# A windowed-attention and FFN kernel: one list scheduler from slot 28 on, with POOL in its model, and the softmax division moved behind the values

## The chip, the cores and the metric

One core of a Trainium2 chip runs the whole program. The metric is the device time of one execution in microseconds; three runs of the kernel before give 895.34 us as median.

The engines are named as the profile names them: PE multiplies matrices and PEld loads its weights, DVE is the vector engine, ACT the scalar (activation) engine, POOL the GpSimd engine, and SP only issues DMAs. Each engine works through its own instruction list strictly in order; an instruction that waits holds up everything behind it on its engine.

## What is computed

```python
# q, k, v: 8 batches x 8 heads x 576 positions x 64
scores = q @ k.T / 8
# heads 0-3 see the last 32 positions, heads 4-7 every 4th of the last 128
scores = where(mask, scores, -1e9)
attn = exp(scores - max); attn = attn / (sum(attn) + 1e-9)
x = (attn @ v) laid out as 4608 tokens x 512
h = x @ w_in                          # 512 x 2048
g = max(h, 0) + log1p(exp(-abs(h)))   # softplus
out = g @ w_out                       # 2048 x 512
```

Everything is float32 to the outside. PE multiplies in a reduced form, so that every operand is split into a high part (a cast, on ACT) and a low part (a subtraction, on DVE) and each product is three matmuls: high x high, low x high, high x low.

## The kernel before

**Tokens and stages.** The 4608 tokens are 9 chunks of 512. Chunks 0 to 2 go through a plain FFN in 48 *slots*: a slot is one 128-wide slice of the 2048 (`ff`) for one chunk, 12 matmuls of w_in (tile `h_ps`), the softplus on ACT and DVE (`e`, then the high part `gh` and the low part `gl`), and, two slots later, 12 matmuls of w_out (tile `o_ps`). `RUNS` sets the order: slots 26 to 31 end chunk 1, slots 32 to 47 are chunk 2. Chunks 3 to 8 go in three *supers* of two chunks each, with Strassen's scheme in the form with seven products: a super is an H half (28 *units* for w_in) and an O half (28 units for w_out), and a unit is 12 matmuls of 128x128x512. The seven products are listed in `PRODUCTS`, named by their left operand: a11, a12 and a22 are blocks of x (or of g in the O half), s1 to s4 are sums of blocks that POOL makes. In an H half the seven products follow one another within each of four column blocks `jj`; in an O half each product runs over the four `jj` before the next begins. Their results go to three pairs of PSUM banks x, y and z, from which ACT and DVE take them (`temp`, `g_of`).

**What an O half costs beside its matmuls.** Each of its 28 units needs its operand split: a cast on ACT (L1100) and a 128x1024 subtraction on DVE (L1181, tile `g`) into one of three pairs of buffers `moving`. For s2, s3 and s4 POOL adds or subtracts a 128x1024 block (L1108), four for each, and four times already in the H half. The weights of a unit come by DMA into a ring of five buffers (`load_unit`).

**Attention.** Two head pairs (a *group* each) make a *couple*; chunk c has the groups 4c to 4c+3, so two couples a chunk, named by the number of their first group. For each group from chunk 2 on: PE makes the scores (`s_ps`), DVE scales, masks and takes the maximum (L380, L385), POOL subtracts the maximum (`shifted`, L388), ACT takes one exponential over 128x512 (L395), DVE sums (L413) and inverts, POOL multiplies by the inverse (`divide`, L421), DVE turns 32x32 squares (L443, `sq`), and SP sends them to DRAM in four DMAs (`turned`) and fetches them back (`pt`). Then PE makes the values (`a_ps`), DVE turns them (L537), and SP sends and fetches x the same way (`rows`, `x_full`). Scores and values share one pair of PSUM banks, and PE takes either as a *visit* of 128 small matmuls.

**Weight jobs.** The sums of weight blocks for the supers are made on the chip: 16 `weight_job`s, each six POOL operations (L818, L834), two casts, two DVE subtractions (L842) and four DMAs (`w_t`).

**What sets the order.** Slots 0 to 9 are written out by hand (`OPENING`). Slots 10 to 47 have a queue of events with due times written by hand (`at`, `attend`, `weight_job`). The supers are ordered by a list scheduler: every piece of work is a `Task` with an engine, a cost and the keys it reads and writes; at each step the engine that can start first runs its most urgent task, by the latest start that its followers allow. POOL is there one more engine; that a POOL operation and a DVE operation can hold each other up is not in the model.

```python
1249            task("DVE", 1.05, gr.divisor, reads=s, writes=[("ri", e)])
1250            task("POOL", 1.05, gr.divide, reads=[("ri", e)], writes=s)
1251            task("DVE", 0.65, turn, n + e, reads=s, writes=[f"q{e}"])
1252            task("SP", 0.4, send, n + e, reads=[f"q{e}"], writes=[("sent", e)], size=QK // 2)
...
1285        done.latest = 5.5 + u * UNIT
```

## Time and profile before

| what | value |
|---|---|
| median of 3 runs | 895.34 us (895.1 to 898.06) |
| the profiled execution, its own time | 893.6 us |
| its span, first to last instruction | 891.8 us |
| PE busy | 829.2 us (93%) |
| DVE busy | 684.6 us (77%) |
| ACT busy | 494.1 us (55%) |
| POOL busy | 344.7 us (39%) |
| mean granted clock of PE | 0.978 |

The last is the share of full speed that the chip granted PE, averaged over the span; where it is 0.50 in a stretch, matmuls run at half their pace. A PE that is drawn as busy need not be at full pace, since the ends of matmuls are modelled. What tells is how long a stage takes for the matmuls in it. The stages, from the span's start: slot 28's first matmul is at 210.2 us, the three H halves begin at 365.2, 548.0 and 728.4, the three O halves at 450.2, 633.7 and 804.5, and the last matmul ends near 887.4.

### The profile page before, as it was taken

To read this page: it belongs to the slowest core of one execution; us is meant where nothing else is said; L and a number is where in the kernel's file an instruction comes from. 1 tells how busy PE (TensorE), PEld (TensorE's weight loads), DVE (VectorE), ACT (ScalarE), POOL (GpSimd) and SP (SyncE) were. 2 spreads that over 40 slices of the span, in tenths; PEclk is the share of its full clock that TensorE was granted. 3 is DMA by queue.
4 is the path that set the end of the run, shared out by engine and by line. 5 is a ranking of instruction groups with operands and counts; after the bars stand their busy time and mean duration, and the time that the engine had idled before them with its cause. 6 is when DMAs were issued, how large, how long until landed. Compare 5 with 4: busy or idle time off the path is not lost.

```text
span 891.8 us, 19364 instructions
## 1 busy us (share of the span) xinstructions
PE 829.2 (93%) x7834; PEld 660.5 (74%) x7835; DVE 684.6 (77%) x872; ACT 494.1 (55%) x767; POOL 344.7 (39%) x218
## 2 busy tenths in 40 slices
PE   6799999899789888999999898899998799999998
PEld 4578888787567776778877676788876588887876
DVE  5798998897586777678799787687896846778663
ACT  5687666555454455467763342586743517775341
POOL 0000101047687879224366342243483502225700
PEclk9899999999899998999999999999999999999999
DMA  9499277989878743897887885969878656664573
GB/s 335 161 354 384 69 212 260 326 252 324 261 245 278 260 152 135 278 343 251 297 286 241 277 295 151 348 215 344 275 255 259 227 199 199 195 190 162 168 239 115
DMA packets 118473, 218.93 MB, mean 245 GB/s; under 512 B 11504, under 2 KB 53616, under 8 KB 118384
## 3 DMA queue, kind: packets, MB, share of 16 engines
q1 hardware_dynamic: 117952, 216.97, 73.1%
q8 instruction: 62, 1.02, 0.5%
q10 hardware_dynamic: 432, 0.72, 0.2%
q14 instruction: 27, 0.22, 0.1%
HBM read 162.07 MB, written 55.57 MB: 244 GB/s over the span
## 4 chain that ended last, share of the span: by engine, by line
PE 62%; DVE 15%; POOL 8%; issue 5%; ACT 5%; DMA 3%; SPq 1%; DVEq 0%; POOLq 0%; ACTq 0%
PE y L208 15%; PE z L208 13%; PE h_ps L208 10%; PE o_ps L208 10%; PE x L208 7%; DVE g L1181 6%; PE s_ps L208 3%; PE a_ps L208 3%; DMA pt<-turned 2%; POOL x_full L878 1%; ACT e L1111 1%; POOL b L818 1%; DVE a_l L890 1%; SPq L143 1%; ACT g L1100 1%
## 5 line engine op out<-in xcount | busy, mean ns | idle before, releaser
L1108 POOL TENSOR_TENSOR g_of<-g_of 128x1024 f32<-128x1024 f32 x36 | 96.5, 2683 | 201.3 <-DVE g_of L1114 179.2
L1181 DVE TENSOR_TENSOR g<-g_of,g 128x1024 fp32r<-128x1024 f32 x72 | 118.2, 1649 | 36.4 <-ACT g L1100 36.4
L208 PE MATMUL h_ps<-xh,parts 128*128 128x512 f32 x384 | 133.2, 404 | 5.6 <-DVE e L655 5.6
L208 PE MATMUL o_ps<-gh,parts 128*128 128x512 f32 x384 | 133.2, 404 | 4.5 <-DVE ob L726 4.2
L1100 ACT CAST g<-g_of 128x1024 fp32r<-128x1024 f32 x72 | 75.4, 1047 | 111.1 <-PE y L208 48.7
L208 PE MATMUL y<-g,ring 128*128 128x512 f32 x432 | 108.9, 406 | 14.5 <-DVE g L1181 14.5
L388 POOL TENSOR_TENSOR s<-s,nm 128x512 f32<-128x512 f32 x28 | 34.9, 1252 | 208.2 <-DVE nm L385 177.1
L208 PEld LDWEIGHTS y<-g,ring 128*128 128x128 f32 x432 | 82.1, 193 | 38.5 <-DVE g L1181 19.7
L1111 ACT ACTIVATE e<-e 128x1024 f32<-128x1024 f32 x96 | 102.0, 1062 | 2.7
L208 PEld LDWEIGHTS h_ps<-xh,parts 128*128 128x128 f32 x384 | 74.3, 193 | 24.1 <-DVE e L655 6.9
L208 PEld LDWEIGHTS o_ps<-gh,parts 128*128 128x128 f32 x384 | 73.5, 191 | 23.3 <-ACT e L649 4.6
L208 PE MATMUL o_ps<-gl,parts 128*128 128x512 f32 x192 | 77.3, 403 | 3.2 <-DVE gl L670 3.2
L208 PE MATMUL h_ps<-xl,parts 128*128 128x512 f32 x192 | 76.8, 400 | 0.0
L208 PE MATMUL z<-g,ring 128*128 128x512 f32 x288 | 70.5, 402 | 5.0 <-DVE g L1181 5.0
L1105 DVE TENSOR_TENSOR temp<-y,temp 128x512 f32<-128x512 f32 x60 | 40.4, 686 | 38.9 <-PE y L208 35.6
L208 PE MATMUL x<-g,ring 128*128 128x512 f32 x288 | 68.4, 395 | 1.0 <-DVE g L1181 1.0
L208 PEld LDWEIGHTS z<-g,ring 128*128 128x128 f32 x288 | 54.6, 191 | 19.6 <-DVE g L1181 6.9
L1114 DVE SCALAR_TENSOR_TENSOR g_of<-g_of,e 128x1024 f32<-128x1024 f32 x36 | 60.8, 1694 | 9.7 <-ACT e L1111 9.5
L208 PEld LDWEIGHTS x<-g,ring 128*128 128x128 f32 x288 | 53.8, 188 | 14.0 <-DVE g L1181 1.4
L208 PE MATMUL x<-a_h,ring 128*128 128x512 f32 x192 | 63.4, 391 | 0.0
L208 PE MATMUL y<-s_h,ring 128*128 128x512 f32 x192 | 63.3, 391 | 0.0
L208 PE MATMUL z<-s_h,ring 128*128 128x512 f32 x192 | 63.2, 390 | 0.0
(94 smaller groups left out, 1634.5 us busy)
## 6 DMA issues: line engine op xcount, KB each, us to landing
ring<-w_t SPq DMA_DIRECT2D x96, 512.0 KB, 4.9
ring<-w_b SPq DMA_DIRECT2D x72, 512.0 KB, 4.3
raw<-w SPq DMA_DIRECT2D x64, 256.0 KB, 5.4
w_t<-cast SPq DMA_DIRECT2D x64, 256.0 KB, 3.4
v<-vp SPq DMA_DIRECT2D x28, 512.0 KB, 5.1
w_b<-parts SPq DMA_DIRECT2D x48, 256.0 KB, 4.6
q<-qp SPq DMA_DIRECT2D x36, 256.0 KB, 5.6
turned<-sq SPq DMA_DIRECT2D x112, 64.0 KB, 2.0
```

What stands on the lines that cost most here:

```text
L143: ins = tc.keep_in_program_order((engine or nc.sync).dma_start(**kw))
L208: tc.keep_in_program_order(nc.tensor.matmul(**kw))
L388: pin(nc.gpsimd.tensor_tensor(out=self.blocks, in0=self.blocks, in1=self.nm.unsqueeze(2).to_broadcast([P, NB, WKEYS]), op=ALU.add))
L818: pin(nc.gpsimd.tensor_tensor(out=sums[j].rearrange("p k n -> p (k n)"), in0=parts[:, 0], in1=parts[:, 1], op=ALU.add))
L878: pin(nc.gpsimd.tensor_tensor(out=dst, in0=a, in1=b, op=op))
L890: pin(nc.vector.tensor_tensor(out=low, in0=x_of(first, name), in1=high.bitcast(F32), op=ALU.subtract))
L1100: pin(nc.scalar.copy(out=dst, in_=src))
L1105: pin(nc.vector.tensor_tensor(out=dst, in0=a, in1=b, op=ALU.add))
L1108: pin(nc.gpsimd.tensor_tensor(out=dst, in0=a, in1=b, op=op))
L1111: pin(nc.scalar.activation(out=dst, in_=src, func=func, **kw))
L1114: pin(nc.vector.scalar_tensor_tensor(out=dst, in0=src, scalar=0.0, in1=e, op0=ALU.max, op1=ALU.add))
L1181: lambda: pin(nc.vector.tensor_tensor(out=low, in0=src, in1=high.bitcast(F32), op=ALU.subtract)),
```

## The change

1. From slot 28 on (`PLANNED`) everything is one list of tasks: the last 20 slots, ten of the weight jobs, the couples and the supers. The due times by hand for that stretch are gone. Two weight jobs stay by hand, and the last four (`LATE_JOBS`) move into the first super. The weight blocks of w_out that are stored unchanged (24 DMAs) move from hand-set times in slots 14 to 28 into the list.
2. The model's costs are new, and a DVE task marked `port` that starts while POOL works is charged up to twice its cost.
3. For all unmasked groups (chunk 2 on) `shifted` and the sum on DVE go; instead ACT takes eight exponentials of 128x64 with the maximum as bias and the sum as accumulated output, as it did for chunks 0 and 1.
4. For couples from 14 on, `divide` on POOL goes; `normalized` multiplies the values by the inverse on DVE, reading PSUM, between the values and their turning.
5. Couples overlap: the scores of a couple are asked for ahead of the values of the one before. From couple 16 on the queries and every second `v` lie in the half of x that the couple will fill, and the fetched squares lie where q lay.
6. The seven products are reordered, s1 second, and the banks with them; in the O half s3 is made in place.

```diff
     PRODUCTS = (
-        ("a11", "b11"), ("s2", "t2"), ("a12", "b21"), ("s3", "t3"), ("s1", "t1"), ("a22", "t4"), ("s4", "b22"),
+        ("a11", "b11"), ("s1", "t1"), ("s2", "t2"), ("a12", "b21"), ("s3", "t3"), ("s4", "b22"), ("a22", "t4"),
     )
...
-        def shifted(self):
-            pin(nc.gpsimd.tensor_tensor(
-                out=self.blocks, in0=self.blocks, in1=self.nm.unsqueeze(2).to_broadcast([P, NB, WKEYS]), op=ALU.add
-            ))
-
-        def exponentials(self):
-            self.sm = wk.tile([P, NB], F32, name="sm")
-            if not self.masked:
-                pin(nc.scalar.activation(out=self.s, in_=self.s, func=AF.Exp))
-                return
-            for t in range(NB):
+        def exponentials(self, some=range(NB)):
+            if 0 in some:
+                self.sm = wk.tile([P, NB], F32, name="sm")
+            for t in some:
...
+        def normalized(self):
...
+            pin(nc.vector.tensor_tensor(
+                out=rows.rearrange("p (h m d) -> p h m d", h=2, d=D),
+                in0=self.rows.rearrange("p h t (r d) -> p h (t r) d", d=D),
+                in1=self.ri.rearrange("p (h m) -> p h m", h=2).unsqueeze(3).to_broadcast([P, 2, 4, D]),
+                op=ALU.mult,
+            ))
...
+    for i in range(OPENED + 1, PLANNED):
...
+    COST = {
+        "PE": 0.2275, "ACT": (0.24, 0.00079), "DVE": (0.16, 0.00104), "POOL": (0.12, 0.00245),
+    }
...
+    @sooner
+    def weights(n, begun=False):
+        x = x_of_couple(n)
+        queries = ["q0", "q1"] if begun else [x]
...
+        Task("PE", 1.4, lambda: scores(n), [*queries, "k0", "k1"], ["att"], visit=True)
+        for e in range(2):
+            gr, s = groups[n + e], both("s") if e == 0 else [("s", 1)]
+            task("DVE", (512, 512), gr.maximum, reads=["att"], writes=s)
+            s = [("s", e)]
+            for t in range(0, NB, 2):
+                Task("ACT", 1.07, lambda gr=gr, t=t: gr.exponentials(range(t, t + 2)), (), s)
...
+    def couples(first, last):
+        for n in range(first, last, 2):
+            weights(n)
+            if n > first:
+                attended(n - 2)
+            turned(n)
+        attended(last - 2)
...
+    for i in range(PLANNED, LAST + 1):
+        if slots[i] == (2, 0):
+            for n in range(BY_HAND, 2 * NPAIR - LATE_JOBS):
+                sooner(job, JOBS_SOONER)(n // NPAIR, n % NPAIR, False)
+        early_slot(i)
+        if slots[i] == (2, LAG):
+            couples(2 * NPAIR, 2 * NPAIR + 4)
...
+            cost = t.cost
+            if t.port and t.engine == "DVE":
+                cost += min(cost, max(0.0, free["POOL"] - start))
```

How the instructions stand, at three places.

POOL, from the last weight job into the halves of the first super; `b` and `d` are a weight job's, `x_full<-x_full` the sums for x of a super, `s<-s,nm` is `shifted`, `s<-s,ri` is `divide`, `g_of<-g_of` the sums of g blocks. Before:

```order
L834 TENSOR_TENSOR b<-b,d 128x256
L834 TENSOR_TENSOR b<-b 128x256
L388 TENSOR_TENSOR s<-s,nm 128x512 x2
L421 TENSOR_TENSOR s<-s,ri 128x512 x2
L1108 TENSOR_TENSOR g_of<-g_of 128x1024 x2
L388 TENSOR_TENSOR s<-s,nm 128x512 x2
L421 TENSOR_TENSOR s<-s,ri 128x512 x2
L1108 TENSOR_TENSOR g_of<-g_of 128x1024 x4
```

After:

```order
L1076 TENSOR_TENSOR b<-parts 128x512 x2
L1076 TENSOR_TENSOR d<-b 128x256 x2
L1076 TENSOR_TENSOR b<-b,d 128x256
L1076 TENSOR_TENSOR b<-b 128x256
L1076 TENSOR_TENSOR b<-parts 128x512 x2
L1076 TENSOR_TENSOR g_of<-g_of 128x1024
L1076 TENSOR_TENSOR d<-b 128x256 x2
L1076 TENSOR_TENSOR b<-b,d 128x256
L1076 TENSOR_TENSOR b<-b 128x256
L1076 TENSOR_TENSOR g_of<-g_of 128x1024 x15
L897 TENSOR_TENSOR x_full<-x_full 128x1024 x4
L1076 TENSOR_TENSOR g_of<-g_of 128x1024 x16
```

The attention's work is gone from POOL, and the last of the jobs (the end of four of them is seen here) lie around the first sum of the first super's H half.

DVE, the last slots before the first unit; `e<-h_ps,e` is the end of a slot's softplus and `gl` its low part, `cast` belongs to weight jobs, `s_l` to the x of the first super. Before:

```order
L655 SCALAR_TENSOR_TENSOR e<-h_ps,e 128x512
L890 TENSOR_TENSOR a_l<-x_full,a_h 128x1024
L842 TENSOR_TENSOR cast<-d,cast 128x2x256
L670 TENSOR_TENSOR gl<-e,gh 128x512
L890 TENSOR_TENSOR s_l<-x_full,s_h 128x1024
L842 TENSOR_TENSOR cast<-b,cast 128x2x256
L890 TENSOR_TENSOR s_l<-x_full,s_h 128x1024
L655 SCALAR_TENSOR_TENSOR e<-h_ps,e 128x512
```

After:

```order
L679 SCALAR_TENSOR_TENSOR e<-h_ps,e 128x512
L694 TENSOR_TENSOR gl<-e,gh 128x512
L1229 TENSOR_TENSOR cast<-b,cast 128x2x256
L679 SCALAR_TENSOR_TENSOR e<-h_ps,e 128x512
L1229 TENSOR_TENSOR cast<-b,cast 128x2x256
L694 TENSOR_TENSOR gl<-e,gh 128x512
L909 TENSOR_TENSOR a_l<-x_full,a_h 128x1024
L679 SCALAR_TENSOR_TENSOR e<-h_ps,e 128x512
L909 TENSOR_TENSOR s_l<-x_full,s_h 128x1024
L694 TENSOR_TENSOR gl<-e,gh 128x512
```

Between `e` and the next `gl` there stood two other subtractions, and now at most one; between two slots' `e`, `gl` apart, there stood five, and now at most two.

DVE, the first super's O half, where the splits `g` of its units alternate with attention. Before:

```order
L1181 TENSOR_TENSOR g<-g_of,g 128x1024
L413 TENSOR_REDUCE sm<-s 128x8
L415 TENSOR_SCALAR sm<-sm 128x8
L418 RECIPROCAL ri<-sm 128x8
L1181 TENSOR_TENSOR g<-e,g 128x1024
L413 TENSOR_REDUCE sm<-s 128x8
L415 TENSOR_SCALAR sm<-sm 128x8
L418 RECIPROCAL ri<-sm 128x8
L443 STREAM_TRANSPOSE sq<-s 128x512
L1181 TENSOR_TENSOR g<-e,g 128x1024
```

After:

```order
L1076 TENSOR_TENSOR g<-g_of,g 128x1024
L536 TENSOR_TENSOR normal<-a_ps,ri 128x512 x2
L449 STREAM_TRANSPOSE sq<-s 128x512 x2
L419 TENSOR_SCALAR sm<-sm 128x8
L424 RECIPROCAL ri<-sm 128x8
L419 TENSOR_SCALAR sm<-sm 128x8
L424 RECIPROCAL ri<-sm 128x8
L1076 TENSOR_TENSOR g<-g_of,g 128x1024
L393 SCALAR_TENSOR_TENSOR s<-s_ps,mask 128x512
L398 TENSOR_REDUCE nm<-s 128x8
```

The sum is gone, the inverse stands behind the turning of the squares instead of ahead of it, and the multiplication `normal` has come in.

## Rows read from the trace of the kernel before

**Rows 1.** E, then H, O alternating: length; busy PE, PEld, DVE, ACT, POOL; clock.
```profile
210.20:365.20 155.00, 136.03 (x1274) 107.39 (x1272) 111.97 (x128) 76.98 (x126) 117.16 (x99) 0.93 0.72 234
365.20:450.20 85.00, 83.29 (x850) 68.30 (x849) 67.66 (x99) 56.91 (x66) 29.61 (x18) 1.00 0.86 286
450.20:548.00 97.80, 88.43 (x849) 68.37 (x849) 87.56 (x73) 41.06 (x44) 51.83 (x22) 0.98 0.75 252
548.00:633.70 85.70, 83.34 (x850) 68.02 (x850) 63.81 (x91) 55.23 (x63) 26.23 (x14) 1.00 0.85 287
633.70:728.40 94.70, 86.24 (x722) 67.94 (x721) 74.06 (x61) 40.37 (x43) 45.91 (x18) 0.98 0.73 246
728.40:804.50 76.10, 76.10 (x337) 63.02 (x336) 50.87 (x61) 52.52 (x59) 14.44 (x6) 1.00 0.63 200
804.50:887.40 82.90, 80.26 (x337) 63.92 (x336) 52.12 (x40) 32.83 (x34) 29.76 (x10) 0.98 0.52 172
```

**Rows 2.** The chain that ended last, one slot's two halves: start, us, what.
```profile
184.51 2.74 PE h_ps L208 x12
187.25 2.80 PE o_ps L208 x12
```

**Rows 3.** PE in order of time, one visit of attention: start, us.
```profile
425.25 1.51 PE L208 MATMUL a_ps<-v,pt 64*32 64x64 f32 x128
```

**Rows 4.** What PE waited for in E: us in total, times, longest.
```profile
PE h_ps L208 <- DVE e L655: 5.6, 2, 3.8
PE a_ps L208 <- DMA pt<-turned: 5.1, 2, 2.9
PE o_ps L208 <- DVE ob L726: 4.2, 1, 4.2
PE o_ps L208 <- DVE gl L670: 3.2, 2, 3.0
```

**Rows 5.** The same, the largest wait in the first and the second O half.
```profile
PE z L208 <- DVE g L1181: 5.0, 2, 3.6
...
PE y L208 <- DVE g L1181: 7.5, 5, 3.0
```

**Rows 6.** One stretch at the lower granted clock, columns of group 1, then DMA.
```profile
818.80:822.10 3.30, 3.30 (x9) 2.62 (x8) 3.30 (x2) 0.00 (x0) 1.41 (x1) 0.50 0.02 7
```

**Rows 7.** DVE's L1181 alone, by stage: first super's O half, last super's H half.
```profile
450.20:548.00 97.80, 48.05 (x25) 0.98 0.75 252
...
728.40:804.50 76.10, 3.65 (x3) 1.00 0.63 200
```

**Rows 8.** DVE in order of time, early in the first O half.
```profile
458.89 3.42 DVE L1181 TENSOR_TENSOR g<-g_of,g 128x1024 fp32r<-128x1024 f32 x1
```

**Rows 9.** POOL in order of time, same half.
```profile
477.26 2.40 POOL L1108 TENSOR_TENSOR g_of<-g_of 128x1024 f32<-128x1024 f32 x1 [1.16 <-DVE g L1181]
```

**Rows 10.** Groups by line: busy us, mean ns, idle before and releaser.
```profile
L388 POOL TENSOR_TENSOR s<-s,nm 128x512 f32<-128x512 f32 x28 | 34.9, 1252 | 208.2 <-DVE nm L385 177.1 <-PE x L208 14.9 <-PE z L208 9.7
L842 DVE TENSOR_TENSOR cast<-d,cast 128x512 fp32r<-128x512 f32 x16 | 19.2, 1200 | 12.6 <-ACT cast L838 12.4
L413 DVE TENSOR_REDUCE sm<-s 128x8 f32<-128x512 f32 x28 | 18.9, 673 | 6.1 <-ACT s L395 5.8
L380 DVE SCALAR_TENSOR_TENSOR s<-s_ps,mask 128x512 f32<-128x512 f32 x28 | 19.0, 678 | 6.4 <-PE s_ps L208 6.4
L395 ACT ACTIVATE s<-s 128x512 f32<-128x512 f32 x28 | 17.2, 626 | 14.5 <-POOL s L388 14.2 <-DMA rows<-turned_x 0.2
```

**Rows 11.** ACT in order of time: first exponential, last accumulator read of a group.
```profile
36.69 0.32 ACT L401 ACTIVATE s<-s_ps,nm 128x64 f32<-128x64 f32 x1
...
38.92 0.25 ACT L401 ACTIVATION_READ_ACCUMULATOR s<-s_ps,nm 128x1 f32 x1
```

**Rows 12.** What SP waited for; the ring's DMA with KB, us to landing.
```profile
SPq L143 <- DVE sq L443: 49.8, 17, 16.7
...
ring<-w_t SPq DMA_DIRECT2D x96, 512.0 KB, 4.9
```

More of the change, by code (lines that the diff above doesn't have):

```diff
@@ L708, in o_part @@
             )
+        return final
+    def o_part(i, m):
+        c, ff = slots[i]
+        resumed = ff == NFF - 1
+        final = o_matmuls(i, m)
+        if m == 0 and final and not resumed:
+            ob_tiles(c)
         if final and resumed:
-            at(now[0] + (3 * STEP if c else 0.12), resumed_part, m, c, o_ps[m], cost=0.69)
-        elif final and c >= FIRST:
-            finished(m, c, o_ps[m])
+            at(now[0] + 0.12, resumed_part, m, c, o_ps[m], cost=0.69)
         elif final and i + LAG <= OPENED:
@@ new lines, in attended @@
+    @sooner
+    def attended(n):
+        x = x_of_couple(n)
+        Task("PE", 1.4, lambda: values(n), ["q0", "q1", *both("v"), x], ["att"], visit=True)
+        for e in range(2):
+            task(
+                "DVE", 512, groups[n + e].normalized, reads=["att", ("ri", e)],
+                writes=both("v") if e == 0 else [("v", 1)],
+            )
+        for e in range(2):
+            task("DVE", 512, groups[n + e].turn_rows, reads=[("v", e)], writes=[x])
+        transfer(groups[n].send_x, reads=[x], writes=["rows"], size=TILE, n=4)
+        transfer(groups[n].bring_x, reads=["rows"], writes=[x], size=TILE)
@@ new lines, in ring_home, with load_ring, h_unit, x_keys @@
+    def ring_home(n):
+        return home_keys(RING_HOMES[n]) + {3: ["C0"], 4: ["C1"]}.get(n, [])
+    def load_ring(u):
+        s, i, k, jj = units[u]
+        b = PRODUCTS[k][1]
+        first = u < RING
+        transfer(
+            load_unit, u, reads=[("D", i, b, 2 * jj + j) for j in range(2)],
+            writes=[("ring", u % RING), *(ring_home(u) if first else ())], size=TILE,
+        )
+    def h_unit(i):
+        for kt in range(NKT):
+            h_part(i, kt)
+    def x_keys(c):
+        return [(f"x{c}", part, k) for part in "hl" for k in range(2)]
@@ new lines, in unit @@
+    def unit(u):
+        _, i, k, jj = units[u]
+        x, b = PRODUCTS[k][0], BANKS[k]
+        begins = k < 3
+        w = ring[u % RING]
+        for n in range(2):
+            dst, m = bank_of(b, n), 0
+            for kk in range(2):
+                for wp, xp in ((0, 0), (0, 1), (1, 0)):
+                    if i == 0:
+                        lhs, rhs = w[:, n, wp, kk * P : (kk + 1) * P], blocks[x][xp][:, kk]
+                        first, final = begins and m == 0, m == 5
+                    else:
+                        lhs, rhs = w[:, kk, wp, n * P : (n + 1) * P], moving[u % 3][xp][:, kk]
+                        first, final = begins and jj == 0 and m == 0, jj == NCP - 1 and m == 5
+                    matmul(out=dst, lhsT=lhs, rhs=rhs, start=first, stop=final, skip_group_check=not begins)
+                    m += 1
@@ new lines, in simulated @@
+            candidates[t.engine].remove(t)
+            order.append(t)
+            cost = t.cost
+            if t.port and t.engine == "DVE":
+                cost += min(cost, max(0.0, free["POOL"] - start))
+            t.begun, end = start, start + cost
+            free[t.engine] = end
+            if t.size:
+                queue_free = max(queue_free, end) + t.size / DMA_RATE
+                end = queue_free + DMA_LATENCY
+            t.done = end
+            for other in t.then:
+                lag = 0.0 if other.engine == t.engine else 1.5 if other.visit else 0.6 if other.engine == "PE" else 0.2
+                other.ready = max(other.ready, end + lag)
+                other.left -= 1
+                if not other.left:
+                    candidates[other.engine].append(other)
@@ new lines, in simulated, with prioritized @@
+        return max(t.done for t in tasks), order
+    def prioritized(begins):
+        for t in tasks:
+            t.latest = END
+        for t, begin in zip(chain, begins):
+            t.latest = begin
+        for t in reversed(tasks):
+            for other in t.then:
+                t.latest = min(t.latest, other.latest - t.tail())
+    ideal, begins = 0.0, []
+    for t in chain:
+        begins.append(ideal)
+        ideal += t.cost * 1.06
+    best = None
+    for _ in range(1):
+        prioritized(begins)
+        end, order = simulated()
+        if best is None or end < best[0]:
+            best = end, order
+        begins = [t.begun for t in chain]
```

666 lines of the change are left out of this document (388 added, 278 removed).

## The prediction

> **What bounds the kernel now.** PE does, but not everywhere at full pace, so I first ask how long each stage would take if PE never waited. The table of stages comes first [rows 1]: each row gives a stage's length, then the busy time of PE, PEld, DVE, ACT and POOL with the number of instructions in brackets, then the granted clock. The H half of the last super has no attention: 337 matmuls in 76.1 us, so 28 units at 2.72 us each with no loss at all. A slot is 2.74 + 2.80 = 5.54 us [rows 2], a visit of attention (128 small matmuls) 1.51 us [rows 3]. Visits are counted from the matmuls: 850 in a half are 336 and four times 128.
>
> Bare lengths and losses then are:
> - E: 20 slots are 110.8, two more w_out parts 5.6, six visits 9.1, together 125.5. It took 155.0, so 29.5 are lost.
> - First super: H 76.1 + 6.0 = 82.1 against 85.0, 2.9 lost; O 82.1 against 97.8, 15.7 lost.
> - Second: H 3.6 lost; O has three visits (722 matmuls), 80.6 against 94.7, 14.1 lost.
> - Third: H none; O 76.1 against 82.9, 6.8 lost.
>
> That is 72.6 us, 29.5 in E, 36.6 in the O halves, 6.5 in the H halves. No faster order can give more.
>
> Next I ask whom PE waited for. In E it was DVE three times out of four: the end of a slot's softplus, its low part, and the addition that frees the `o_ps` banks, 13.0 us, and the fetched squares of attention, 5.1 [rows 4]. In the O halves it was DVE's split `g` [rows 5]. After such waits the granted clock falls to 0.50, the lower of its two levels (1.2 of 2.4 GHz): in 3.3 us nine matmuls start [rows 6] where 14.5 would at 0.227 each, so a dip costs about 1.25 us more. The low clock in E's mean (0.93 of 155 us, so 22 us at half) is worth some 10 of the 29.5.
>
> Why is DVE late? Not through its own work: the split takes 3.65 / 3 = 1.22 us where POOL is quiet and 48.05 / 25 = 1.92 in the first O half [rows 7], single ones 3.42 [rows 8], which is 1.22 beside a POOL sum of 2.40 [rows 9]: a DVE operation with two SBUF inputs and a POOL operation take turns. The excess over 25 splits is 48.05 − 30.5 = 17.6 us, more than that half lost. DVE is busy 87.6 of 97.8 there, but only 52.1 of 82.9 in the third O half, which lost 6.8 all the same: there the order and the turns with POOL cost, not the sum of the work.
>
> **The change part by part.** *POOL and attention.* 28 `shifted` and 22 `divide` of the same shape leave POOL: 28 x 1.25 = 35 us [rows 10] and, at that price, 27 more. The sums on DVE go, 28 x 0.67 = 18.8; `normalized` is new to the trace. Its nearest row is L380, one PSUM input and one from SBUF at the same width, 0.68 [rows 10]: 22 x 0.68 = 15. Bounds: 0.68 to 1.22, the split's price, so 15 to 27. I take 15, since the operands are L380's. DVE's own load stays as it is. None of this is on PE's path by itself; it counts in DVE's turns with POOL. An O half held on average some eight of these POOL operations, 10 us, and DVE loses between none of that and all of it: I take 5 in the first two.
>
> *Eight exponentials for one.* From the first start at 36.69 to the end of the last read at 39.17 a group takes 2.48 us on ACT [rows 11] against 0.63 [rows 10], 28 x 1.85 = 52 us more. Upper bound, if nothing overlapped: 8 x (0.32 + 0.25) = 4.6. ACT has room in O (41.1 of 97.8) and E (77 of 155). In an H half it is at 56.9 of 85 with six groups; with six at 2.48 it would be 68, at 4.6 it would be 81 of 82, full. So H loses between nothing and 10 us more; I take 2 for all H halves, with the last four jobs (eight subtractions at 1.2 [rows 10], in a half where DVE is at 67.7) inside it.
>
> *The list for E.* The three waits on DVE there arise because a fixed order put the softplus behind subtractions that took two to three times what was allowed. The new order leaves at most two of them between two slots' softplus, where there were five. Attention's values get six slots after their scores (couple 14: slots 28 and 34, before 27 and 31), so the 5.1 us on fetched squares should go; with these gaps go the dips. But DVE stays as full as before: 112 of 155 us now; without 10 of the 30 subtractions of weight jobs there (12 us), 100 of some 136. Bounds for the loss that is left: 4 (the ends, two short gaps) and 24 (the same share as now). I take 10, so −19.5.
>
> *The list for the O halves.* POOL's turns are now charged to DVE, and s1, which POOL has finished in the H half, is multiplied second, so POOL has four more units (10.9 us) before the first block of s2 is needed. Operations that take turns in such a half: 16 sums x 2.40 = 38.4 on POOL and 35 splits x 1.22 = 42.7 on DVE, 81.1 together, where PE needs 82.1. The turns alone nearly fill the half, so it cannot run without loss unless DVE's other work falls into POOL's turns. Bounds: no loss (gain 36.6), and only the 5 + 5 for the missing POOL work. I take half: 15.7, 14.1 and 6.8 become 8, 7 and 4, so −17.6. The model's surcharge stops at twice the cost, 2.44; the row of 3.42 is a microsecond over it, the mean of 1.92 under it.
>
> The Trainium skill, SBUF — State Buffer, section Who interferes with whom, says that the pair of ports which the two engines share is an exclusive lock and that the loser blocks for the whole instruction. By it every split that starts just behind a 2.40 us sum is later than the list believes; with half of 35 so caught the lateness is 17 us in an O half and its gain is gone (the first rival below). The trace agrees in the single case (3.42), and its mean says that most are caught less.
>
> *Before slot 28.* DVE's sum and POOL's shift go for six groups there, and fewer weight stores crowd the squares' DMA, for which PE waits there too; between 0 and the longest such wait, 2.9 [rows 4], I take −1. *DMAs.* The same bytes move in less time; PE never waits on the ring in the trace, so nothing is charged.
>
> Sum, on the profiled execution's 893.6: −19.5 − 17.6 + 2 − 1 = −36.1, so 857.5. The median of the runs shown lies 1.7 above that execution, so **859 us**.
>
> **The rivals.**
> - *Turns with POOL stay the bound of the O halves.* The O halves give only half of the 10 us of POOL work each, about 6 in all, and E, where POOL's ten jobs fill the same turns, only 10. For it: 81.1 of 82.1. Against: the third O half lost 6.8 with DVE half idle, so order counts. 893.6 − 16 + 1 + 1.7 = 880.
> - *Nearly all losses go.* If E keeps 5 and each O half 2 to 4, the gain is 52: about 842. For it: the H half without a loss, made by the same sort of list. Against: DVE's load in E.
> - *The list does not do what it says.* Real times differ from the model's (an exponential pair is charged 1.07 where 0.62 is seen), the in-order lists wait elsewhere, and the sum is nothing: 890 to 898.
> - *Slower: SP's one queue.* Every couple has three sends that hold SP until DVE is done, and the ring's loads stand behind them. SP waited 49.8 us in 17 pieces for the squares already, the longest 16.7, and a ring load lands 4.9 us after its issue [rows 12]. The ring is at most four units, 10.9 us, ahead, so a send that waits over 6 us starves PE, and with a clock dip each such place costs some 3.7. There are 33 such places; at ten the forecast gain is gone, at fourteen the time is 859 + 52 = 911. Against it: the same sends stand in the same queue now, and no wait of PE names the ring.
>
> **How the numbers follow.** Forecast (848 to 870) 0.50; turns with POOL (870 to 889) 0.19; nearly all gone (835 to 848) 0.12; nothing gained 0.08; slower 0.11. Of "nothing gained", 0.06 lies within 0.3% of before (892.7 to 898), which is about what a measurement of this kernel can tell from no change; 0.02 goes to each side. Faster: 0.50 + 0.19 + 0.12 + 0.01 = 0.82; same 0.06; slower 0.12. The range runs from 840 to 893: it leaves out the slower case and part of the fast one, together under 2 in 10. The bounds of the unknown costs (E 4 to 24, O 0 to 27, H +10) lie inside or at its ends.
>
> **What would show it.** E right: slot 28's first matmul to the first unit in 130 to 140 us, no PE wait on L679, L694 or L1302 over 2 us, and few dips. O right: halves of 85 to 92 us, DVE's split (now L1076) below 1.8 us on average in them. ACT: a group's eight exponentials in about 2.5 us, H halves not over 87. The forecast is wrong if the O halves still take 95, if PE waits for the ring, or if an H half is held by ACT.

## The result and the profile after

The changed kernel takes 864.5 us (858.8 to 865.9, four runs) where the kernel before takes 895.2: a ratio of 0.964, interval 0.959 to 0.969. Run again beside the first experiments it had 860.9 us, 0.962 (0.958 to 0.966). The profiled execution took 864.9 us, 28.7 less than that of before, and 27.8 of these lie ahead of the last matmul's end (887.4 there, 859.6 here).

The stage windows of the changed kernel, columns as in [rows 1] (E, then H and O alternating):

```profile
212.90:353.20 140.30, 130.58 (x1146) 103.85 (x1145) 87.42 (x117) 85.02 (x207) 74.69 (x64) 0.96 0.79 259
353.20:432.70 79.50, 79.50 (x593) 65.55 (x592) 63.38 (x85) 63.09 (x112) 40.94 (x30) 1.00 0.91 305
432.70:531.20 98.50, 90.62 (x1105) 71.42 (x1104) 79.25 (x84) 51.89 (x123) 36.48 (x13) 0.98 0.83 281
531.20:615.60 84.40, 83.80 (x850) 67.97 (x848) 69.17 (x87) 67.20 (x126) 24.97 (x9) 1.00 0.84 285
615.60:703.80 88.20, 86.25 (x849) 69.22 (x848) 75.57 (x75) 47.61 (x102) 39.38 (x13) 0.98 0.88 295
703.80:780.10 76.30, 76.30 (x338) 63.02 (x337) 56.12 (x66) 54.29 (x61) 17.77 (x8) 1.00 0.61 202
780.10:859.60 79.50, 78.84 (x337) 62.66 (x335) 56.42 (x39) 32.85 (x34) 31.45 (x10) 1.00 0.52 180
```

Lengths alone mislead here, because the visits have moved: by the matmul counts (336 of units and 128 a visit) the first super now has two visits in H and six in O, where it had four and four; E has five for six, the second O half four for three. So the bare lengths are worked out anew, by the prediction's prices, and the losses compared:

| stage | loss before | bare after | length after | loss after | gained |
|---|---|---|---|---|---|
| E | 29.5 | 123.9 | 140.3 | 16.4 | 13.1 |
| first super, H | 2.9 | 79.1 | 79.5 | 0.4 | 2.5 |
| first super, O | 15.7 | 85.2 | 98.5 | 13.3 | 2.4 |
| second, H | 3.6 | 82.1 | 84.4 | 2.3 | 1.3 |
| second, O | 14.1 | 82.1 | 88.2 | 6.1 | 8.0 |
| third, H | 0 | 76.1 | 76.3 | 0.2 | −0.2 |
| third, O | 6.8 | 76.1 | 79.5 | 3.4 | 3.4 |
| sum | 72.6 | | | 42.1 | 30.5 |

Slot 28 begins 2.7 us later (212.9), so 30.5 − 2.7 = 27.8.

What PE waited for in E, and then in all supers, columns as in [rows 4]:

```profile
PE o_ps L211 <- DVE gl L694: 4.0, 2, 3.7
PE h_ps L211 <- DVE e L679: 3.9, 2, 3.0
PE a_ps L211 <- DMA sq<-turned: 1.0, 2, 0.5
...
PE x L211 <- DVE g L1076: 5.8, 3, 2.0
PE y L211 <- DVE g L1076: 3.1, 3, 2.6
PE z L211 <- DMA ring<-w_b: 1.3, 2, 0.8
```

In E two large waits are left where [rows 4] has four of 2.9 or more. DVE also has less to do there: it is busy 87.4 us where it was 112.0, and the prediction reckoned with 100. One reason is that the weight jobs' subtractions are fewer, another that they now take 0.74 us each, 1.2 before [rows 10]:

```profile
L1229 DVE TENSOR_TENSOR cast<-b,cast 128x512 fp32r<-128x512 f32 x20 | 14.7, 740 | 11.5 <-ACT cast L1225 11.5
```

DVE's splits `g` alone, in the three O halves (length; busy and count; clock):

```profile
432.70:531.20 98.50, 39.22 (x25) 0.98 0.83 281
615.60:703.80 88.20, 41.06 (x25) 0.98 0.88 295
780.10:859.60 79.50, 47.64 (x25) 1.00 0.52 180
```

In the first half a split takes 39.22 / 25 = 1.57 us against 1.92 [rows 7]. In the third it takes 1.91, and yet that half lost 3.4 us, the least of the three. A long split is not by itself a late one.

### The profile page after: what moved, and what is told of

The parts are those of the page before. It is cut to its first block, busy times and chain, and to the rows that moved or that the text cites. A ratio compares the mean times of both kernels' runs of the same rounds, so it can differ in the third digit from the quotient of the medians.

```text
span 863.1 us, 19689 instructions
## 1 busy us (share of the span) xinstructions
PE 820.5 (95%) x7834; PEld 656.8 (76%) x7835; DVE 654.9 (76%) x866; ACT 551.8 (64%) x1187; POOL 288.5 (33%) x168
## 4 chain that ended last, share of the span: by engine, by line
PE 72%; DVE 10%; DMA 8%; ACT 4%; issue 3%; SPq 2%; DVEq 0%; ACTq 0%
PE y L211 20%; PE x L211 13%; PE z L211 12%; PE h_ps L211 11%; PE o_ps L211 10%; DVE g L1076 3%; PE s_ps L211 3%; PE a_ps L211 2%; SPq L146 2%; ACT s L407 2%; DMA w_t<-cast 1%; DMA pt<-turned 1%; DMA ring<-w_b 1%; DVE s_l L909 1%; DMA x_full<-rows 1%
## 5 line engine op out<-in xcount | busy, mean ns | idle before, releaser
L1076 POOL TENSOR_TENSOR g_of<-g_of 128x1024 f32<-128x1024 f32 x48 | 141.9, 2969 | 198.9 <-DVE g_of L1389 123.9
L1076 DVE TENSOR_TENSOR g<-g_of,g 128x1024 fp32r<-128x1024 f32 x84 | 144.1, 1726 | 39.5 <-ACT g L1083 39.2
L1083 ACT CAST g<-g_of 128x1024 fp32r<-128x1024 f32 x84 | 87.6, 1046 | 103.5 <-PE y L211 36.3
L211 PE MATMUL y<-g,ring 128*128 128x512 f32 x432 | 105.6, 401 | 3.2 <-DVE g L1076 3.1
L407 ACT ACTIVATE s<-s,nm 128x64 f32<-128x64 f32 x224 | 74.8, 336 | 24.2 <-DVE nm L398 23.1
L211 PE MATMUL x<-g,ring 128*128 128x512 f32 x288 | 71.0, 403 | 5.8 <-DVE g L1076 5.8
L211 PE MATMUL z<-g,ring 128*128 128x512 f32 x288 | 68.7, 395 | 1.3 <-DMA ring<-w_b 1.3
L1076 POOL TENSOR_TENSOR b<-parts 128x512 f32<-128x512 f32 x28 | 41.7, 1500 | 73.5 <-DVE cast L1229 72.4
L427 POOL TENSOR_TENSOR s<-s,ri 128x512 f32<-128x512 f32 x6 | 6.8, 1136 | 176.1 <-ACT parts L202 101.7
```

The source lines that it names most:

```text
L211: tc.keep_in_program_order(nc.tensor.matmul(**kw))
L407: pin(nc.scalar.activation(out=self.blocks[:, t], in_=src, func=AF.Exp, bias=self.nm[:, t : t + 1], scale=1.0 / 8.0 if self.masked else 1. ...
L427: pin((engine or nc.gpsimd).tensor_tensor(out=self.blocks, in0=self.blocks, in1=self.ri.unsqueeze(2).to_broadcast([P, NB, WKEYS]), op=ALU. ...
L1076: pin(engine_of(name).tensor_tensor(out=dst, in0=a, in1=b, op=op))
L1083: pin(nc.scalar.copy(out=dst, in_=src))
```

## Experiments

Lengths of the stages in each profiled execution, from the first matmul of a stage to the first of the next, with the visits in brackets; "slot 28" is where E begins, "losses" their sum by the same prices, and the ratio is that of the runs to the kernel before, with its interval.

| kernel | slot 28 | E | H1 | O1 | H2 | O2 | H3 | O3 | losses | ratio |
|---|---|---|---|---|---|---|---|---|---|---|
| before | 210.2 | 155.0 (6) | 85.0 (4) | 97.8 (4) | 85.7 (4) | 94.7 (3) | 76.1 | 82.9 | 72.6 | 1 |
| x_before_charge | 211.9 | 155.2 (6) | 84.6 (4) | 92.5 (4) | 84.4 (4) | 93.4 (3) | 76.2 | 81.9 | 63.4 | 0.989 (0.985 to 0.992) |
| after | 212.9 | 140.3 (5) | 79.5 (2) | 98.5 (6) | 84.4 (4) | 88.2 (4) | 76.3 | 79.5 | 42.1 | 0.964 (0.959 to 0.969) |
| x_after_again | 209.9 | 141.2 (5) | 79.7 (2) | 97.6 (6) | 83.0 (4) | 88.2 (4) | 76.2 | 79.5 | 40.8 | 0.962 (0.958 to 0.966) |
| x_cap_off | 210.9 | 142.7 (5) | 79.9 (2) | 94.5 (6) | 83.8 (4) | 88.2 (4) | 76.5 | 79.5 | 40.4 | 0.960 (0.957 to 0.963) |
| x_no_charge | 209.6 | 141.0 (5) | 80.5 (2) | 99.2 (6) | 86.1 (4) | 91.0 (4) | 76.3 | 79.5 | 48.9 | 0.971 (0.968 to 0.975) |
| x_no_add | 213.7 | 143.9 (5) | 79.7 (2) | 94.7 (6) | 83.1 (4) | 87.1 (4) | 76.5 | 79.5 | 39.8 | 0.959 (0.956 to 0.962) |
| x_seam | 210.5 | 142.5 (5) | 79.9 (2) | 96.9 (6) | 84.4 (4) | 88.2 (4) | 76.2 | 79.5 | 43.0 | 0.965 (0.963 to 0.967) |
| x_divide_back | 208.3 | 142.2 (5) | 81.2 (3) | 92.8 (5) | 82.8 (4) | 89.0 (4) | 76.2 | 79.5 | 39.0 | 0.963 (0.960 to 0.966) |
| x_one_exp | 208.5 | 137.7 (5) | 79.5 (2) | 98.4 (6) | 83.1 (4) | 88.1 (4) | 76.2 | 79.5 | 37.7 | 0.958 (0.956 to 0.960) |
| x_s2_second | 209.7 | 138.7 (5) | 79.5 (2) | 96.1 (6) | 79.6 (2) | 91.0 (6) | 76.2 | 78.4 | 34.7 | 0.956 (0.953 to 0.958) |
| x_apart | 208.0 | 134.1 (5) | 85.4 (3) | 105.9 (5) | 95.2 (3) | 98.2 (5) | 76.3 | 79.5 | 69.9 | 0.992 (0.989 to 0.995) |
| x_all_undone | 207.9 | 137.5 (5) | 79.8 (2) | 100.4 (6) | 90.7 (5) | 84.3 (3) | 76.2 | 78.4 | 42.5 | 0.964 (0.960 to 0.967) |
| x_seam_queue | 208.0 | 131.2 (5) | 79.5 (2) | 98.2 (6) | 88.7 (5) | 87.1 (3) | 76.2 | 78.4 | 34.6 | 0.951 (0.948 to 0.954) |

**The changed kernel again.** 

> The changed kernel unaltered, as the measure for the three others on the same chip. Expected 0.962 to 0.968 of before (860 to 866 us), as in its first runs. If the time before slot 28 (2.7 us longer than before in the first profile, with the clock at 0.78 in the first 14 us) is a matter of the execution and not of the kernel, this profile has it at 209 to 211 us.

860.9 us. Slot 28 begins at 209.9 here, and between 208.0 and 212.9 in the eight profiles that share the same first 28 slots: the 2.7 us are of the execution, not of the change. The stages repeat within 1.5 us.

**The charge for POOL's turns, dropped and made full.**

```diff
-                cost += min(cost, max(0.0, free["POOL"] - start))
+                cost += 0.0                                  # x_no_charge
+                cost += max(0.0, free["POOL"] - start)       # x_cap_off
```

> The model charges DVE nothing for POOL's turns; all else is the changed kernel. Theory 1 (knowing POOL's turns is a good part of what the O halves gained, 14 us): 4 to 10 us slower than the changed kernel, the loss in the three O halves and the mean split there back toward 1.9 us. Rival (order, product sequence and the missing POOL work made the gain, the surcharge little): within 2 us.

868.9 us, 8.0 more than the changed kernel on the same chip; theory 1 holds for the time. Its place was only in part as expected: the losses grow by 1.5 us in the first O half, 2.8 in the second and 3.0 in the second H half, and not at all in the third O half and in E. And its means of the split were 41.31 / 25 = 1.65 and 38.10 / 25 = 1.52 us, no worse than with the charge. So the charge does not make the turns shorter, and without it the mean does not go back toward 1.9, as theory 1 had it.

> The model charges a DVE operation that starts while POOL works with all of what POOL's operation has left, not with at most its own cost again. Theory 1 (DVE loses a whole POOL operation at a turn: in the changed kernel a low part of 0.69 us took 2.82 beside POOL's sums, charged as 1.4): the list keeps short DVE operations out of POOL's long rows, the 3.7 us wait on a low part at 345 us and part of the first O half's 13 us go, 2 to 6 us faster than the changed kernel. Theory 2 (the mean split of 1.73 us is what counts and twice the cost covers it): within 2 us of the changed kernel.

860.6 us, the same, as theory 2 had it. The first O half is 3.1 us shorter, E 1.5 longer. The wait on the low part is still there: in the changed kernel, DVE in order of time, then ACT's cast and POOL's row beside it (start, us):

```profile
342.79 0.68 DVE L679 SCALAR_TENSOR_TENSOR e<-h_ps,e 128x512 f32<-128x512 f32 x1
343.39 2.82 DVE L909 TENSOR_TENSOR s_l<-x_full,s_h 128x1024 fp32r<-128x1024 f32 x1
346.14 2.82 DVE L694 TENSOR_TENSOR gl<-e,gh 128x512 fp32r<-128x512 f32 x1
...
343.56 0.62 ACT L688 CAST gh<-e 128x512 fp32r<-128x512 f32 x1 [0.69 <-DVE e L679]
...
339.05 12.13 POOL L897 TENSOR_TENSOR x_full<-x_full 128x1024 f32<-128x1024 f32 x4 [5.06 <-DMA w_t<-cast]
```

POOL has four sums in a row, DVE gets in between two of them, and the low part `gl` (0.69 us alone) could have begun at 344.2, when its high part is cast, and is 4.1 us late at its end: 1.9 behind `s_l`, which DVE had taken meanwhile, and 2.1 for its own turn. With the right price in the model the order at this place is the same (the wait is 3.6 there). That list starts whatever is ready first; a price cannot tell it to leave DVE idle for the urgent piece.

**The smallest operation.**

```diff
         def divisor(self):
-            pin(nc.vector.tensor_scalar(
-                out=sm, in0=sm, scalar1=1.0e-9, scalar2=1.0, op0=ALU.add, op1=ALU.mult
-            ))
```

> Leaves out the addition of 1e-9 to the sums (128x8 numbers, 36 times), which the inverse follows at once. Theory 1: this smallest DVE operation (0.16 us alone) waits for a whole POOL operation: 2.37 and 2.20 us in a row in the first O half, ahead of the largest wait of PE there (2.58), 2.35 in the second. Without it about 9 us of DVE time go, and 2 to 4 us of the whole. Rival: the next DVE operation in the list takes the same turn in its place, and the time stays within 1.5 us.

859.1 us; its interval overlaps that of the changed kernel, so the time decides nothing. In the profile the first O half is 2.9 us shorter than in x_after_again, which would fit theory 1, and E is 2.7 longer in this execution. This is the place in the changed kernel, DVE in order of time, then two of POOL's sums beside it:

```profile
450.98 2.20 DVE L1076 TENSOR_TENSOR g<-g_of,g 128x1024 fp32r<-128x1024 f32 x1
453.11 2.37 DVE L419 TENSOR_SCALAR sm<-sm 128x8 f32<-128x8 f32 x1
455.51 0.20 DVE L424 RECIPROCAL ri<-sm 128x8 f32<-128x8 f32 x1
455.63 2.20 DVE L419 TENSOR_SCALAR sm<-sm 128x8 f32<-128x8 f32 x1
457.87 0.20 DVE L424 RECIPROCAL ri<-sm 128x8 f32<-128x8 f32 x1
...
452.05 3.40 POOL L1076 TENSOR_TENSOR g_of<-g_of 128x1024 f32<-128x1024 f32 x1
455.41 2.40 POOL L1076 TENSOR_TENSOR g_of<-g_of 128x1024 f32<-128x1024 f32 x1
```

An addition over eight columns waits twice for a sum of POOL: the two end at 455.48 and 457.83, the sums beside them at 455.45 and 457.81. PE's largest wait in the supers (2.6) follows at 458.7. The list charged it 0.34 together with the inverse, and no turn. The whole gain of this edit is not settled beyond "0 to 4 us".

**The seam.**

```diff
+    held = tasks[-1]                  # the low part of x of chunk 2, second half
...
-            t.left, t.ready = len(t.after), 0.0
+            t.left, t.ready = len(t.after), 11.0 if t is held else 0.0
```

> One low part (for x of chunk 2, the first DVE task of the list that reads nothing of it) may not start before 11 us of the model's time. In all four profiles of the changed list DVE stood 5.8 to 6.6 us at this instruction, just behind slot 28, until the results of chunk 0 had gone out of the tile that it overwrites; that store was issued by the part with due times, so the list does not know it. Theory 1 (this wait holds the maxima, the exponentials and so the softplus that PE then waits for, 3.0 to 5.4 us, with a clock dip): stretch E gets 3 to 6 us shorter and no wait of over 2 us is left near 220 us; 0.956 to 0.959 of before. Rival (ACT's exponentials ahead of the softplus hold PE, whenever they run): the wait moves by a slot, and the time is within 1.5 us of the changed kernel.

863.3 us: no gain, and E is no shorter (142.5). In the changed kernel the chain at the seam was this, DVE and then ACT in order of time with the idle time ahead and what ended it:

```profile
221.28 1.22 DVE L280 TENSOR_TENSOR xl<-x_full,xh 128x1024 fp32r<-128x1024 f32 x1 [5.76 <-DMA out_t<-ob]
...
223.86 0.35 ACT L407 ACTIVATE s<-s,nm 128x64 f32<-128x64 f32 x1 [8.11 <-DVE nm L398]
```

In x_seam that wait is gone, DVE does the maxima at 213 us, and the softplus holds PE for 0.9 us only. But PE then waits ahead of couple 14's values (x_seam, PE's waits in E):

```profile
PE a_ps L211 <- issue: 4.2, 1, 4.2
...
PE a_ps L211 <- DMA sq<-turned: 3.2, 3, 1.7
```

The profile names nothing that ended the 4.2 us, but they end at 246.8, some 4 us after the fetch of the first squares was issued (242.5), so I count them with the wait on the second squares (1.7). SP of the same kernel in order of time shows why the squares were late:

```profile
220.58 2.05 SPq L146 DMA_DIRECT2D ob<-kept  x4
...
224.09 8.04 SPq L146 DMA_DIRECT2D w_b<-parts  x10
...
234.87 3.03 SPq L146 DMA_DIRECT2D turned<-sq  x4
```

The first squares were turned by 224.7 us and sent at 234.9, behind 13 stores of weight blocks. The rival's reason (ACT's order) is not what the rows show; the wait went into SP's queue. The list had SP free at slot 28, while its first transfer (`ob<-kept`) was issued 10 us later.

**The division back on POOL.**

```diff
+            task("POOL", 512, groups[n + e].divide, reads=[("ri", e)], writes=[("s", e)], port=True)
             task("DVE", 512, turn, n + e, ...)
...
-            task("DVE", 512, groups[n + e].normalized, ...)
```

> The division by the sums goes back to POOL, between the inverse and the turning of the squares, for the 22 groups from couple 14 on; the multiplication on DVE behind the values goes. POOL gets 22 operations of 1.04 us or more, DVE loses 22 of 0.68. Theory 1 (turns with POOL are what the O halves lose by): 3 to 8 us slower than the changed kernel, in E and the first two O halves. Rival (DVE's sum of work is the bound, and a list that knows POOL hides the turns): the 15 us that DVE saves outweigh them, 0 to 4 us faster.

860.6 us, as the changed kernel: not theory 1, and the lower end of the rival's 0 to 4. The exchange, 22 operations more on POOL for 22 fewer on DVE, changes nothing that can be measured in a list that knows them; what POOL's operations alone would cost is not told apart. The two O halves together lose 16.1 us against 18.5 in x_after_again, with a visit moved out of the first.

**One exponential again.**

```diff
-            for t in range(0, NB, 2):
-                Task("ACT", 1.07, lambda gr=gr, t=t: gr.exponentials(range(t, t + 2)), (), s)
+            task("POOL", 512, gr.shifted, writes=s, port=True)
+            task("ACT", 512, gr.exponentials, writes=s)
...
-            task("DVE", (8, 8), groups[n + e].divisor, ...)
+            task("DVE", (512, 8, 8), groups[n + e].divisor, ...)
```

> The scores again have the maximum subtracted on POOL, one exponential over 128x512 on ACT and the sum on DVE, for all 28 groups from chunk 2 on; the division stays behind the values. POOL gets 28 operations of 1.04 us or more, DVE 28 of 0.67, and ACT loses some 50 us of work. Theory 1 (turns and DVE bound): 5 to 10 us slower than the changed kernel, half of it in E and the first two O halves. Rival (ACT's eight exponentials stand in front of softplus and casts, and cost as much): within 2 us.

856.6 us, ratio 0.958 (0.956 to 0.960): not slower, rather 4 to 5 us faster than the changed kernel, whose two ratios are 0.962 and 0.964, though the intervals still touch. Theory 1 misses the sign, and the rival's 2 us are exceeded. The first two O halves are those of the changed kernel (98.4 and 88.1), with six of POOL's 28 operations in them. E is 2.6 to 3.5 us shorter, but that cannot be put down to the exponentials alone: E is 138.7 in x_s2_second below, which keeps all eight, and this edit also alters the part ahead of slot 28. In the changed kernel a group's exponentials took 0.34 us each with their read, eight of them 2.7:

```profile
477.65 0.35 ACT L407 ACTIVATE s<-s,nm 128x64 f32<-128x64 f32 x1 [0.41 <-DVE nm L398]
477.90 0.19 ACT L407 ACTIVATION_READ_ACCUMULATOR s<-s,nm 128x1 f32 x1
478.00 0.33 ACT L407 ACTIVATE s<-s,nm 128x64 f32<-128x64 f32 x1
```

**The order of the products.**

```diff
-        ("a11", "b11"), ("s1", "t1"), ("s2", "t2"), ...
+        ("a11", "b11"), ("s2", "t2"), ("s1", "t1"), ...
...
-    BANKS = "xzyxyzy"
+    BANKS = "xyzxyzy"
```

> s2 is multiplied second and s1 third, as s2 was second before the change; the banks and temporary sums are swapped with them, all else is the changed kernel. POOL has four units (10.9 us) less before the first sum s2 of an O half is needed. Theory 1 (that lead is part of what the O halves gained, and the only change that the third one got beside the list's charge): each O half loses 1 to 3 us more, 3 to 8 us together, the third one back to some 82 us. Rival (the list makes the sums of s2 in the H half in either order): within 2 us, the third O half at 79.5.

854.6 us. In this kernel the sums for x follow the new order too, so that s2 of an H half is made of the block as it stands before s1 is added to it: one of seven operands holds other numbers, so that this kernel does not compute the result that is asked for, and it does not wait for s1. Theory 1 has the sign wrong, and the rival's 2 us are exceeded. The third O half, where no attention is, takes 78.4 us against 79.5, and so in both later kernels with this order: the lead of s1 bought nothing there, it cost 1.1. The rest of the gain comes with other places of the visits (two in the second H half and six in the O half behind it), and whether that is due to the order or to the wait that is missing is not told by this run.

**The charge alone, in the kernel before.**

```diff
-    ... WHOLE = {"DVE": 1.23, "ACT": 0.94, "POOL": 2.0}
+    ... WHOLE = {"DVE": 1.23, "ACT": 0.94, "POOL": 2.63}
...
-        end = free[t.engine] = start + t.cost
+        cost = t.cost
+        if t.engine == "DVE" and cost == WHOLE["DVE"]:
+            cost += min(cost, max(0.0, free["POOL"] - start))
+        end = free[t.engine] = start + cost
```

> The kernel before, with one edit to the list of its supers: a DVE operation over 128x1024 that starts while POOL works is charged up to twice its cost, and POOL's sum is charged 2.63 in place of 2.0, both as in the changed kernel. Stretch E is as before (155 us). Theory 1 (the charge is a gain of its own, about the 8 us that leaving it out cost the changed kernel): 4 to 9 us faster than before (0.990 to 0.995), all of it in the three O halves. Rival (the charge only helps a list that can move things, with couples that overlap and POOL freed of attention): within 2 us of before.

884.5 us, 10.0 less: theory 1 holds, a little above its 4 to 9. In the profiles the losses fall by 9.2 us, 7.6 of them in the O halves. The edit holds two prices, the charge and POOL's 2.63, which were not tried apart. DVE's L1181 in the three O halves of this kernel:

```profile
451.70:544.20 92.50, 51.64 (x25) 0.98 0.79 266
628.60:722.00 93.40, 46.54 (x25) 0.98 0.73 249
798.20:880.00 81.80, 41.23 (x25) 1.00 0.51 174
```

The first half is 5.3 us shorter while its splits take 51.64 us against 48.05 [rows 7]. What falls is PE's wait for them in that half, here from the kernel before and then from x_before_charge:

```profile
PE z L208 <- DVE g L1181: 5.0, 2, 3.6
PE y L208 <- DVE g L1181: 4.4, 5, 1.3
...
PE y L208 <- DVE g L1181: 3.6, 3, 1.9
```

So the charge does not lessen the turns; by these waits, the list places the splits so that PE sees less of them.

**Couples that don't overlap.**

```diff
         for n in range(first, last, 2):
             weights(n)
-            if n > first:
-                attended(n - 2)
             turned(n)
-        attended(last - 2)
+            attended(n)
```

> The couples no longer overlap in the list's program: the values of a couple are asked for before the scores of the next one; the buffers and all else are the changed kernel. Theory 1 (the overlap gives each couple's squares time to come back, which the first H half's two visits and E's short waits show): the visits move later, 4 to 25 us slower than the changed kernel, most of it where PE waits for squares. Rival (one couple at a time fits into the time of a super anyway): within 2 us.

887.8 us, ratio 0.992 (0.989 to 0.995): 25 to 27 us slower than the changed kernel by the ratios, the largest effect of all. It is the price of the overlap in this list, whose buffers are laid out for it. E is even shorter (134.1), but the first O half loses 22 us by the prices above, the second super 14.6 in each half. PE's largest waits in its supers:

```profile
PE z L211 <- DVE g L1076: 13.0, 3, 6.3
PE z L211 <- ACT s_h L905: 8.0, 1, 8.0
PE z L211 <- ACT g L1083: 7.2, 2, 4.6
```

SP, then ACT, in order of time around the start of the second H half:

```profile
528.47 2.58 SPq L146 DMA_DIRECT2D rows<-x_full  x4
...
534.09 0.32 SPq L146 DMA_DIRECT2D x_full<-rows  x1
...
540.63 1.04 ACT L905 CAST a_h<-x_full 128x1024 fp32r<-128x1024 f32 x1 [3.71 <-DMA x_full<-rows]
```

The half began at 533.4 (first matmul), and the last couple's x came back from DRAM some 7 us after that. PE does not wait for squares, as the expectation had it. At this place it is the end of the chain that is late, the last couple's x and the sums and casts of x that follow it: PE's 8.0 us end at 544.3, and of the half's 14.6 these and a wait of 2.5 right behind them are 10.5. The waits in the O halves are others: there PE waits for splits and their casts. The longest, 6.3 us, ends at 461.9, and ahead of its split DVE has a turn of 3.36 us and then the scaling and maxima of a couple's scores (458.0 to 460.7):

```profile
454.72 3.36 DVE L1076 TENSOR_TENSOR g<-g_of,g 128x1024 fp32r<-128x1024 f32 x1
...
460.64 2.35 DVE L1076 TENSOR_TENSOR g<-g_of,g 128x1024 fp32r<-128x1024 f32 x2
```

Why the list without overlap puts them so is not shown.

**What did no harm, together.** x_one_exp, the order of x_s2_second with the sums of x left as in the changed kernel, and x_no_add; like x_no_add it leaves out the 1e-9 of the formula.

> The changed kernel with what undoing did not harm: maximum subtracted on POOL, one exponential and the sum on DVE (as x_one_exp), s2 multiplied second and s1 third in both halves (the sums of x still made in the order s1, s2, so that all products have their operands), and the 1e-9 left out. Theory 2, formed after those runs (the list with its charge makes the gain, the eight exponentials and s1 second cost): the gains of x_one_exp (4 us) and x_s2_second (6) add up, 850 to 853 us, 0.949 to 0.953. Rival (x_s2_second was fast because its s2 did not wait for s1, or because visits fell elsewhere): 855 to 858, as x_one_exp.

861.2 us, 0.964 (0.960 to 0.967), as the changed kernel. The gains do not add up: E keeps its three us (137.5), the third O half its one, but the visits fall otherwise, five in the second H half, which now loses 7.1. Theory 2 falls in its size, and the rival's 855 is missed too.

**The seam with SP's backlog.** The same kernel with two numbers more:

```diff
+        free["SP"] = 10.0
...
-            t.left, t.ready = len(t.after), 0.0
+            t.left, t.ready = len(t.after), 11.0 if t is held else 0.0
```

> The kernel of x_all_undone, and at the seam to the list the low part of x held until 11 us (as x_seam) and SP free only from 10 us of the model's time, since in the traces SP issued the list's first transfer some 10 us after slot 28. Theory 1 (x_seam gained nothing because the squares' sends of couple 14 then stood behind 13 stores of weight blocks in SP's list): with both corrected neither the softplus nor the squares hold PE at slots 30 to 34, and E is 3 to 7 us shorter than in x_all_undone. Rival (the DMA queue is full there, 0.9 to 1.0 busy, so what goes first only changes who is late): within 1.5 us.

850.8 us, 0.951 (0.948 to 0.954): 10.4 us less than x_all_undone, and faster than both kernels. E is 6.3 us shorter, and its granted clock rises from 0.96 to 0.99 (columns as in [rows 1]; x_all_undone first):

```profile
207.90:345.40 137.50, 129.63 (x1148) 103.61 (x1146) 94.58 (x119) 72.76 (x117) 83.23 (x72) 0.96 0.81 268
```

and x_seam_queue:

```profile
208.00:339.20 131.20, 126.70 (x1149) 102.11 (x1145) 89.68 (x117) 71.37 (x116) 77.55 (x71) 0.99 0.85 279
```

The one wait of PE that is left there is 4.5 us for a low part, up to 335.0 us. In x_all_undone PE waited 4.4 us for the same, and at the seam for the softplus, which is gone:

```profile
PE h_ps L211 <- DVE e L686: 2.3, 1, 2.3
```

For squares it waited only 0.3 us there, since couple 14's first squares were sent at 224.5 already, behind three stores. So what can be seen of the gain in E is at the softplus; what the sends add is not told. SP in order of time shows them ahead of the stores now:

```profile
220.26 4.41 SPq L146 DMA_DIRECT2D turned<-sq  x8
...
227.56 0.95 SPq L146 DMA_DIRECT2D w_b<-parts  x2
```

The same transfers fitted into 6.3 us less (a DMA share of 0.85 for 0.81), so the queue was not the bound that the rival made it. Beside E the first super's O half and the second's H half gain 2 us each, and the O half behind loses 2.8; the two profiled executions differ by less (7.9 us at the last matmul) than the medians.

## Why the prediction came out, and where its steps did not

The time, 864.5 and 860.9 us, lies in the forecast's own case (848 to 870; 859 named). Its steps fared less well, and that the sum held is in part luck: E and the O halves gave 10.2 us less than forecast and the H halves 5.6 more, the overlap, which costs most when it is undone, had almost no price, and two of the three grounds for the O halves show no gain.

- **E, −19.5; measured −13.1.** The sign was right, the size off: a loss of 10 was allowed, 16.4 was left. The upper bound of 24 was also too low: "the same share as now" of the bare length would be 29. The length (140.3) just misses 130 to 140, and "no wait on L679, L694 over 2 us" was wrong twice (3.0, 3.7). The 3.0 is at the seam: the list does not know what the hand-ordered part left running. With that put in, on top of the edits of x_all_undone, x_seam_queue has 131.2 us and loses 7.3, near the 10 allowed. That the new order made the gain is argued from these waits alone: neither the charge nor the overlap did (141.0 and 134.1 us without them), but no run parts the order from the four weight jobs that left E.
- **O halves, −17.6; measured −13.8** (2.4, 8.0, 3.4). The size is near, though not half by half: the first still takes 98.5 us where 85 to 92 were named as the sign and 95 as the sign of being wrong (95.5 with the two visits that it has more left out). Of the reasons, "the 5 + 5 for the missing POOL work" is nothing that can be seen: x_divide_back has eleven such operations in the first two halves and the same time, x_one_exp six and a better one, each with its exchange on DVE. The eight POOL operations that the 5 was taken from were also those of the first half alone; the second had four. "POOL's turns are now charged to DVE" is right: 8 us when dropped, of which 4.3 lie in the O halves, and 10 when given to the kernel before. "POOL has four more units before s2" gave nothing in the third half. I judged by the sum of the turns (81.1 of 82.1), and that sum was wrong: its 16 sums are those of a whole super, and an O half has 10, with 4 for x in the first two, so some 76 us there and 57 in the third (10 x 2.40, and 27 operations on DVE at 1.22). It was the wrong measure too: x_before_charge is faster with longer splits. My sign "splits below 1.8" was met in two halves and says little.
- **What I priced too low** is the overlap of the couples. It stood in the text only with the 5.1 us of E; undone, it costs 25 to 27 us, in the halves of the first two supers and not in E, which is shorter without it. Together with the charge that is more than the whole gain: the parts are not additive.
- **H, +2; measured −3.6** (2.5, 1.3, −0.2 gained). The eight exponentials take 2.7 us a group, near the 2.48, and ACT is at 67.2 of 84.4. The H halves had room for them. The whole pays some 4 to 5 us for them (x_one_exp); where is not shown. `normalized` took the 0.68 that was reckoned for it.
- **Before slot 28, −1.** Not to be told: eight profiles of the same code spread over 4.9 us there.
- **The charge's cap.** I had the row of 3.42 a microsecond over the cap and the mean under it. Charging all of it changed nothing in the whole (0.960 against 0.962). The Trainium skill's rule (SBUF — State Buffer, Who interferes with whom) that the loser blocks for the whole instruction is borne out by the smallest operation, 2.37 us for eight columns, which ends as POOL's sum does; its consequence as I had put it, a gain that goes in the O halves, did not come.
- **The slower rival** did not come either: PE waited 1.3 us for the ring in all. Something near it is real: in x_seam sends stood behind stores in SP's queue.
- **The chances.** Of "nothing gained", 0.08 less 0.06 leaves 0.01 for each side, not 0.02; the sums that follow have it right.

Open: what shortens the third O half from 82.9 to 79.5 us. It is not the overlap (79.5 without), not s1 second (78.4 without), and the charge gives 1 us in the kernel before and nothing in the changed one (79.5 without); prices, places of buffers or s3 in place were not tried apart. Open too: how much of x_seam_queue is SP's ten microseconds alone, since that edit was not run without the other, and what of E's gain is the list's.

## What to carry to other kernels

When a list scheduler is extended, first give it what the part ahead leaves behind (which tiles are still being read, when each queue is really free): two numbers at the seam were worth 10 us here, and one of them alone nothing (x_seam). Judge a chain that must be ready for the next stage by when its last piece arrives, not by the load on any engine. Operations that another engine lengthens need not cost anything on the path: with the wait in the schedule's prices the kernel before got 10 us faster while its splits got longer, so the sum of such lengthening is no forecast of the time.

## What the runs showed of the hardware

- A `tensor_scalar` over 128x8, 0.17 us in the median of its 36, took 2.37 and 2.20 beside POOL's sums, while the reciprocal over the same 128x8 between them kept its 0.20. The Trainium skill (SBUF — State Buffer, Who interferes with whom) names `tensor_scalar` among the operations that can contend for the shared pair; that much agrees.
- POOL pays as well: its sum takes 2.40 us alone [rows 9], and 2.97 on average over the 48 of the changed kernel:

```profile
L1076 POOL TENSOR_TENSOR g_of<-g_of 128x1024 f32<-128x1024 f32 x48 | 141.9, 2969 | 198.9 <-DVE g_of L1389 123.9
```
